# Local attention in 32-query tiles with 128 keys each, and global attention as separate tasks, in a fused attention and feed-forward kernel

## The chip, the core and the metric

The kernel runs on one core of one Trainium2 chip. The metric is the device time of one execution in microseconds. The three timed runs of the kernel before took 1042.81, 1039.39 and 1042.66 us, so the median is 1042.66 us.

## The reference, cut to what matters

There are 8 batches with 8 heads of 64 numbers each. Every head has 512 local tokens and 32 global tokens. A local query sees the 32 global keys and the local keys at most 32 positions away; a global query sees all 544 keys. The concatenated heads of the 4,352 tokens then go through a feed-forward layer of width 512 to 2048 to 512.

```python
s_g = scale * np.matmul(q_g, k_all.transpose(0, 1, 3, 2))
out_g = np.matmul(sm(s_g), v_all)                # global queries: all keys
mask = np.abs(pos[:, None] - pos[None, :]) <= 32
s_ll = np.where(mask, scale * q_l @ k_l.T, -1e9)
s_l = np.concatenate([s_lg, s_ll], axis=-1)      # 32 global keys, then local
out_l = np.matmul(sm(s_l), np.concatenate([v_g, v_l], axis=2))
h = x @ w_in                                     # x: heads side by side
g = np.maximum(h, 0.0) + alpha * np.minimum(h, 0.0)
out = g @ w_out
```

## The kernel before

**Feed-forward.** The tokens are cut into nine groups: one for the 512 local tokens of each batch, and a last one with the 256 global tokens. A group has 16 units, one for each 128 of the 2048 hidden numbers. A unit is `f1` (12 matmuls, the products of activations and weights split into a high and a low fp32r part, into a bank of tag `h`) and `f2` (12 matmuls into the four banks `o0` to `o3`, two units later, `LAG`). Between them DVE makes `g` (L407, L408), ACT its high part `gh` (L410) and POOL its low part `gl` (L411). After unit 16 ACT copies the four banks out.

**Weights.** They arrive as fp64 words. Each of 32 pieces is decoded by two ACT, three DVE (L115, L117, L118) and one POOL instruction (L120), then split by a DVE or ACT copy (L127, L129) and a POOL subtraction (L130). All pieces are decoded once, beside the attention of the first batches.

**Attention.** A pair `P` is two heads of one batch, so a batch has four pairs and there are 32 in all. A pair takes four units of the program. Pairs 0 to 7 (`NRAW`) use fp32 score matmuls of 64 queries by 160 keys (`qk_raw`), with PE transposes (L316). Pairs from 8 on use split fp32r scores with 128 queries by 192 or 224 keys (`hi`, `kl`): DVE adds the mask and takes the extreme (L246), ACT exponentiates (L250) and scales (L217), DVE transposes blocks of 32x32 (L327), and the probabilities are written to a scratch tensor in DRAM and fetched back transposed (`scratch`, `pt_sb`).

**Global queries.** The 64 global rows of a pair ride with the local ones. `global_scores` makes three matmuls per pair (`g_ps<-gn`). `global_softmax` has nine small DVE and two ACT instructions. `global_transposes` puts the result into `pt_sb` beside the local probabilities (L300, L301: 18 DVE transposes per pair from pair 8 on), so that the value matmuls of the next visit (`pv_all`, with 160 or 128 columns) give local and global outputs together.

**What sets the order.** The main loop runs over `t` from -`NPRE` = -19 to 145, and `u = t + NPRE` counts from 0. In each unit the attention pieces stand at three places: `attn_pre` ahead of `f1`, `attn_mid` between `f1` and `f2`, `attn_post` between the halves of `f2`. A scheduler orders each engine's instructions within priorities. From `u >= PIN` (36) TensorE's matmuls stay in program order. PSUM has eight banks: two of tag `h`, two of tag `s` (all attention of the later pairs) and `o0` to `o3`.

```python
for t in range(-NPRE, NT + LAG):
    ...
    attn_pre(u)
    if 0 <= t < NT: f1(t)
    attn_mid(u)
    if t >= LAG: f2(t - LAG, 0)
    attn_post(u)
    if t >= LAG: f2(t - LAG, 1)
    weights_step(u)
```

Of the kernel before, what the change touches and what calls it, by code (L numbers as in the profile page):

```python
# [17 lines left out]
NPAIR = 4  # L18
# [3 lines left out]
NQ, NK = 512, 640  # L22
NEG = -8.0e9
NKR = 704
PEC = "ad"
PEG = "da"
NWARM = 18
WARM = (2, 2)
NRAW = 8
WV = range(0, 8)  # L30
NWB = 33
NST = 18
NNP = [(0, 0), (0, 2)]
# [7 lines left out]
NPRE = 19  # L41
PIN = 36
LAG = 2
PTT = "s"
BT = dict(s="s", g="o3", o="s", w="h")
GS = (2, "mid")
EV = dict(pt0=(2, "mid"), pt1=(4, "pre"), ptg=(4, "pre"), pv0=(5, "mid"), pv1=(6, "mid"))
SM = (2, "post")
RATE = ((1, 1, 0), (2, 1))
GROUPS = [("l", b) for b in range(NB)] + [("g", 0)]  # L50

# [7 lines left out]

@with_exitstack  # L60
def longformer_ffn(ctx: ExitStack, tc: tile.TileContext, qk, qkr, gn, vt, vx, w, alpha, out):
# [35 lines left out]

    def stage(name, dtype=F32):
        return work.tile([128, 512], dtype, tag="st", name=name, bufs=NST)

    wraw, wts = {}, {}
# [4 lines left out]

    wmid = {}
# [15 lines left out]
    def split_weights(f, j):  # L123
        t = wmid.pop((f, j))
        wt = wpool.tile([128, 2, 512], F32R, tag="w", name="wt")
        if f in WV:
            nc.vector.tensor_copy(wt[:, 0, :], t)  # L127
        else:
            nc.scalar.copy(wt[:, 0, :], t)  # L129
# [10 lines left out]
    nc.vector.memset(rmask[0:64, 0, 0:32], NEG)  # L140
    nc.vector.memset(rmask[64:128, 2, 128:160], NEG)

    ident = stage("ident")[:, 0:128]
    make_identity(nc, ident)

    idle = stage("idle", F32R)
    nc.vector.memset(idle.bitcast(F32), 0.0)

    def keep_warm(n):
        for _ in range(n):  # L150
# [54 lines left out]
    def small(name, n=2):  # L205
        return work.tile([128, n], F32, tag=name, name=name, bufs=3)
# [453 lines left out]
```

## Time and profile before

| what | value |
|---|---|
| timed runs, median | 1042.66 us |
| profiled execution, first to last instruction | 1038.9 us |
| PE busy | 992.1 us, 96% of the span, 5592 matmul records |
| DVE busy | 681.0 us, 66% |
| ACT busy | 497.4 us, 48% |
| POOL busy | 410.6 us, 40% |
| moved by DMA | 133.00 MB, 128 GB/s in the mean |
| TensorE clock granted, mean | 0.977 |

The profiled execution's own time is its span, 1038.9 us; the median of the timed runs is 3.8 us above it. A matmul in fp32 shows as two records of the trace, a matmul in fp32r as one. Matmuls overlap in the trace, so the time that one costs is read from the starts of neighbours, not from its own duration. "L93" is the helper through which every matmul is issued; tiles tell them apart: `h_ps` is `f1`, `o` is `f2`, `s_ps` local scores, `o_ps` values, `g_ps` the bank that holds global scores and the last piece of the values. A PE row is named by the matmul that it belongs to, and PEld is the load of its stationary operand.

### The profile page before, as it was taken

To read this page: it belongs to the slowest core of one execution; us is meant where nothing else is said; L and a number is where in the kernel's file an instruction comes from. 1 tells how busy PE (TensorE), PEld (TensorE's weight loads), DVE (VectorE), ACT (ScalarE), POOL (GpSimd) and SP (SyncE) were. 2 spreads that over 40 slices of the span, in tenths; PEclk is the share of its full clock that TensorE was granted. 3 is DMA by queue.
4 is the path that set the end of the run, shared out by engine and by line. 5 is a ranking of instruction groups with operands and counts; after the bars stand their busy time and mean duration, and the time that the engine had idled before them with its cause. 6 is when DMAs were issued, how large, how long until landed. Compare 5 with 4: busy or idle time off the path is not lost.

```text
span 1038.9 us, 17103 instructions
## 1 busy us (share of the span) xinstructions
PE 992.1 (96%) x5592; PEld 791.2 (76%) x5592; DVE 681.0 (66%) x2162; ACT 497.4 (48%) x1331; POOL 410.6 (40%) x330
## 2 busy tenths in 40 slices
PE   6798989898999999999999999999999999999998
PEld 3455767676888878887888788878887788888798
DVE  8987788866666766676667666776667666322322
ACT  5466466665455554455455554555455543201121
POOL 6620466663344343333444433334443431122222
PEclk9896898998999999999999999999999999999999
DMA  9454232135444554455455555445445543100010
GB/s 335 175 187 172 103 126 86 56 94 161 148 148 141 160 149 148 140 161 157 148 149 151 165 150 148 141 149 151 148 144 159 146 126 92 41 1 1 1 42 21
DMA packets 95274, 133.00 MB, mean 128 GB/s; under 512 B 10192, under 2 KB 53712, under 8 KB 95184
## 3 DMA queue, kind: packets, MB, share of 16 engines
q1 hardware_dynamic: 95184, 131.91, 40.7%
q8 instruction: 44, 0.72, 0.3%
q14 instruction: 46, 0.38, 0.1%
HBM read 100.93 MB, written 30.93 MB: 127 GB/s over the span
## 4 chain that ended last, share of the span: by engine, by line
PE 77%; DVE 14%; DMA 3%; ACT 2%; issue 2%; POOL 1%; SPq 0%; ACTq 0%; DVEq 0%; POOLq 0%
PE o L93 33%; PE h_ps L93 31%; PE o_ps L93 6%; PE s_ps L93 4%; PE g_ps L93 3%; DVE wt L118 2%; DVE wt L115 2%; DVE rz L211 1%; DVE wt L117 1%; DMA rawq<-in_qk_dram 1%; DVE p_sb L246 1%; DVE g L408 1%; DMA out_dram<-ost 1%; DVE g L407 1%; DVE pt_sb L321 1%
## 5 line engine op out<-in xcount | busy, mean ns | idle before, releaser
L93 PE MATMUL h_ps<-xh,wt 128*128 128x512 f32 (+1 forms) x1152 | 352.2, 389 | 4.3 <-DVE g L408 3.9
L411 POOL TENSOR_TENSOR gl<-g,gh 128x512 fp32r<-128x512 f32 (+1 forms) x144 | 178.2, 1237 | 436.8 <-ACT gh L410 405.1
L93 PE MATMUL o<-gh,wt 128*128 128x512 f32 (+1 forms) x1152 | 282.4, 386 | 1.6 <-ACT ost L305 1.6
L93 PEld LDWEIGHTS o<-gh,wt 128*128 128x128 f32 x1152 | 204.5, 188 | 50.3 <-ACT ost L305 6.6
L93 PEld LDWEIGHTS h_ps<-xh,wt 128*128 128x128 f32 x1152 | 207.3, 191 | 44.6 <-DVE g L408 4.1
L93 PE MATMUL h_ps<-xl,wt 128*128 128x512 f32 (+1 forms) x576 | 222.6, 388 | 0.9 <-DVE xl L390 0.9
L410 ACT CAST gh<-g 128x512 fp32r<-128x512 f32 (+1 forms) x144 | 85.9, 596 | 266.4 <-DVE g L408 243.2
L407 DVE TENSOR_SCALAR g<-h_ps,alpha_sb 128x512 f32<-128x512 f32 (+1 forms) x144 | 103.2, 717 | 121.2 <-PE h_ps L93 120.4
L217 ACT ACTIVATE p_sb<-p_sb,rz 128x192 f32<-128x192 f32 (+1 forms) x252 | 101.3, 451 | 131.8 <-DVE rz L212 129.7
L93 PE MATMUL o<-gl,wt 128*128 128x512 f32 (+1 forms) x576 | 150.6, 382 | 0.0
L250 ACT ACTIVATE p_sb<-p_sb,mn 128x224 f32<-128x224 f32 (+2 forms) x256 | 115.0, 451 | 40.3 <-DVE mn L246 39.8
L93 PEld LDWEIGHTS h_ps<-xl,wt 128*128 128x128 f32 x576 | 109.3, 190 | 25.6 <-issue 1.3
L93 PEld LDWEIGHTS o<-gl,wt 128*128 128x128 f32 x576 | 104.5, 187 | 23.8 <-issue 0.5
L211 DVE TENSOR_SCALAR rz<-z 128x2 f32<-128x2 f32 x128 | 52.5, 411 | 91.3 <-ACT p_sb L250 90.2
L300 DVE STREAM_TRANSPOSE pt_sb<-sg_sb 32x64 f32<-32x64 f32 x384 | 90.7, 236 | 27.4 <-ACT sg_sb L283 21.2
L408 DVE SCALAR_TENSOR_TENSOR g<-h_ps,g 128x512 f32<-128x512 f32 (+1 forms) x144 | 93.9, 652 | 2.9
L196 POOL TENSOR_TENSOR hi<-rawq,hi 64x512 fp32r<-64x512 f32 x48 | 62.2, 1295 | 83.4 <-DMA vt<-in_vt_dram 50.0
L93 PE MATMUL o_ps<-pt_sb,vt 128*64 128x160 f32 (+4 forms) x832 | 72.3, 298 | 11.9 <-DVE mn L246 8.0
L199 POOL TENSOR_TENSOR kl<-rawk,hi 128x640 fp32r<-128x640 f32 x48 | 76.2, 1587 | 3.7
L93 PEld LDWEIGHTS o_ps<-pt_sb,vt 128*64 128x64 f32 (+2 forms) x832 | 50.3, 140 | 32.5 <-issue 12.2
L246 DVE CUSTOM_DVE_ANT_0 p_sb<-s_ps,mask 128x192 f32<-128x192 f32 x192 | 64.1, 362 | 11.1 <-PE s_ps L93 9.9
L120 POOL TENSOR_TENSOR wt<-wt,wr 128x512 int32<-128x512 int32 x32 | 43.2, 1352 | 66.2 <-DVE rz L211 38.1
(86 smaller groups left out, 1042.3 us busy)
## 6 DMA issues: line engine op xcount, KB each, us to landing
scratch<-p_sb SPq DMA_DIRECT2D x192, 112.0 KB, 2.3
wraw<-in_w_dram SPq DMA_DIRECT2D x32, 512.0 KB, 6.9
vt<-in_vt_dram SPq DMA_DIRECT2D x32, 512.0 KB, 5.0
rawk<-in_qk_dram SPq DMA_DIRECT2D x96, 160.0 KB, 2.9
rawq<-in_qk_dram SPq DMA_DIRECT2D x96, 128.0 KB, 2.7
pt_sb<-scratch SPq DMA_DIRECT2D x48, 256.0 KB, 2.8
gn<-in_gn_dram SPq DMA_DIRECT2D x32, 304.0 KB, 5.4
pt_sb<-scratch SPq DMA_DIRECT2D x48, 192.0 KB, 2.9
```

Of the source, the lines that this page charges most:

```text
L93: ins = nc.tensor.matmul(*a, **k)
L196: nc.gpsimd.tensor_tensor(q, raw[64:128], q.bitcast(F32), op=ALU.subtract)
L199: nc.gpsimd.tensor_tensor(kl[P, h], raw, t.bitcast(F32), op=ALU.subtract)
L211: nc.vector.tensor_scalar(rz[:parts, 0:n], z[:parts, 0:n], 1e-9, None, op0=ALU.add)
L217: nc.scalar.activation(r, r, AF.Copy, scale=rz[:parts, e : e + 1])
L246: nc.vector.tensor_tensor_reduce(out=pr, in0=s[:, 256 * e : 256 * e + nn], in1=masks[e], scale=-0.125, scalar=3.0e38, op0=ALU.add, op1=ALU ...
L250: nc.scalar.activation(pr, pr, AF.Exp, bias=mn[:, e : e + 1], scale=-1.0, accum_out=z[:, e : e + 1])
L300: nc.vector.transpose(dst, src)
L407: nc.vector.tensor_scalar(g[:, 0:n], h[:, 0:n], 0.0, alpha_sb[:, f : f + 1], op0=ALU.min, op1=ALU.mult)
L408: nc.vector.scalar_tensor_tensor(g[:, 0:n], h[:, 0:n], 0.0, g[:, 0:n], op0=ALU.max, op1=ALU.add)
L410: nc.scalar.copy(gh[:, 0:n], g[:, 0:n])
L411: nc.gpsimd.tensor_tensor(gl[:, 0:n], g[:, 0:n], gh[:, 0:n].bitcast(F32), op=ALU.subtract)
```

## The change

The attention is written anew; the feed-forward functions `f1` and `f2` stay as they are (`f1` is now at L279, its DVE lines at L291 and L292, ACT L294, POOL L295).

Local attention of every pair now works on blocks of 32 queries with the 128 keys that start at `window(i)` of a re-laid key sequence: 32 fp32 matmuls with 64x32 tiles per pair, one head in rows 0 to 63 and the other in rows 64 to 127 of the array, each head into its own bank (`s_ps`). The softmax runs on 128x512 tiles; eight PE transposes of 128x128 follow two units later, and 32 value matmuls (128 keys, 64 numbers, 32 queries) one unit after that. The fp32r split of queries and keys and the DRAM scratch go. Key and value blocks are laid out by the host and loaded by one and two DMAs per pair.

Global attention is a task of its own: scores and softmax (`global_scores`) between `f1` and `f2` of unit 16 + 17k/5 for pair `k`, and two units later, at the same place, `global_values`: two PE transposes, a DVE copy, two small DVE transposes (L265) and ten value matmuls.

The first batch's four pairs start every two units from `t = -10`; the weights are decoded at half a piece per unit before `t = 0` and at two pieces per unit from there on, in another order.

```diff
-NRAW = 8
...
-NPRE = 19
-PIN = 36
+NPRE = 10
+PIN = 16
...
-        if P < NRAW:
-            vxs[P] = stage("vx").rearrange("p (i n) -> p i n", i=4)
-            nc.sync.dma_start(vxs[P], vx[P])
+    def load_qk(P):
+        qks[P] = work.tile([128, SL + KS], F32, tag="qk", name="qk", bufs=2)
+        nc.sync.dma_start(qks[P], qk[P])
...
+    def local_scores(P):
+        t = qks.pop(P)
+        tags = ("o0", "o1", "o2", "o3") if P < NPAIR else ("s", "s", "s", "s")
+        for h in range(2):
+            ps_of[P, h] = bank(tags[2 * (P % 2) + h], "s_ps")
+        for i in range(NWIN):
+            for h in range(2):
+                hs = slice(64 * h, 64 * h + 64)
+                k0 = SL + window(i)
+                r0, c0 = 32 * (i % 4), 128 * (i // 4)
+                matmul(ps_of[P, h][r0 : r0 + 32, c0 : c0 + 128], t[hs, 32 * i : 32 * i + 32], t[hs, k0 : k0 + 128], start=True, stop=True)
+    def local_softmax(P):
+        for h in range(2):
+            s = ps_of.pop((P, h))
+            p = stage("p")
+            p3 = p.rearrange("q (i n) -> q i n", i=4)
+            mn, z, rz = small("mn"), small("z"), small("rz")
+            nc.vector.scalar_tensor_tensor(p, s, -0.125, mask.rearrange("q i n -> q (i n)"), op0=ALU.mult, op1=ALU.add)
+            nc.vector.tensor_reduce(mn, p3, axis=AX.X, op=ALU.min)
+            for i in range(4):
+                nc.scalar.activation(p3[:, i], p3[:, i], AF.Exp, bias=mn[:, i : i + 1], scale=-1.0, accum_out=z[:, i : i + 1])
+            nc.vector.tensor_scalar(rz, z, 1e-9, None, op0=ALU.add)
+            nc.vector.reciprocal(rz, rz)
+            eng = nc.gpsimd if P < NPAIR and h == 0 else nc.vector
+            eng.tensor_tensor(p3, p3, sub_ap(rz, 0, 128, 0, ((1, 4), (0, 128))), op=ALU.mult)
+            pr_of[P, h] = p
+    def local_transposes(P):
+        for h in range(2):
+            p = pr_of.pop((P, h))
+            ps = bank("s", "pt")
+            for i in range(4):
+                transpose(ps[:, 128 * i : 128 * i + 128], p[:, 128 * i : 128 * i + 128], ident)
+            pt_of[P, h] = stage("pt")
+            copy("ad"[h], pt_of[P, h], ps)
+    def local_values(P):
+        b, p = divmod(P, NPAIR)
+        o = bank("h" if P < NPAIR else "s", "o_ps")
+        for i in range(NWIN):
+            v = vws[P, i % 2][:, i // 2]
+            for h in range(2):
+                q = slice(32 * i, 32 * i + 32)
+                matmul(o[64 * h : 64 * h + 64, q], v[:, 64 * h : 64 * h + 64], pt_of[P, h][:, q], start=True, stop=True)
+        if P < NPAIR:
+            xs[0, p] = split(o, SL)
+        else:
+            nc.scalar.copy(x_raw[:, p], o)
...
-    def transpose_q(h):
-        pr = p_sb[:, 896 * h : 896 * h + 896]
-        nc.vector.transpose(pr, pr)
...
-    def fetch_pt(h):
...
+    def global_values(P):
+        b, p = divmod(P, NPAIR)
+        ps = bank("s", "gt")
+        for e in range(2):
+            transpose(ps[:, 128 * e : 128 * e + 128], sg_sb[:, 128 * e : 128 * e + 128], ident)
+        nc.vector.tensor_copy(sgt_sb[:, 0:4].rearrange("k (r e) n -> k r e n", r=2), ps[:, 0:256].rearrange("k (e r n) -> k r e n", e=2, r=2))
+        for h in range(2):
+            nc.vector.transpose(sgt_sb[0:32, 4, 32 * h : 32 * h + 32], sg_sb[32 * h : 32 * h + 32, 256:288])
+        v = vgs.pop(P)
+        for y in range(5):
+            for h in range(2):
+                matmul(ps[64 * h : 64 * h + 64, 256:288], v[:, y, 64 * h : 64 * h + 64], sgt_sb[:, y, 32 * h : 32 * h + 32], start=(y == 0), stop=(y == 4))
+        nc.scalar.copy(x_glb[:, p, SG * b : SG * b + SG], ps[:, 256:288])
...
+    for P in range(NPR):
+        base = 2 * P - NPRE if P < NPAIR else 4 * (P - NPAIR)
+        plan(base, "pre", local_scores, P)
+        plan(base, "pre", local_softmax, P)
+        plan(base + 2, "pre", local_transposes, P)
+        plan(base + 3, "pre", local_values, P)
...
+    for k in range(NPR):
+        t = 16 + (17 * k) // 5
+        plan(t - 2, "post", load_global, k)
+        plan(t, "mid", global_scores, k)
+        plan(t + 2, "mid", global_values, k)
...
-        weights_step(u)
+        weights_step(2 if t >= 0 else u % 2 if u < NPRE else 1)
```

The prediction speaks of two places in the order that results. The first is on PE, in the units from `t = 16` on, where the global task meets the feed-forward stream. Before, this is the visit of one pair's values with the next pair's global scores (`o_ps`, `g_ps`), between the `h_ps` of one unit and the `o` (accumulators `o0` to `o3`, with their buffer number) of another:

```order
L93 MATMUL h_ps<-xl,wt 128x512
L93 MATMUL o_ps<-pt_sb,vt 64x160 x2
L93 MATMUL o_ps<-pt_sb,vt 64x128 x2
L93 MATMUL o_ps<-pt_sb,vt 64x160 x2
L93 MATMUL o_ps<-pt_sb,vt 64x128 x2
L93 MATMUL o_ps<-pt_sb,vt 64x160 x2
L93 MATMUL o_ps<-pt_sb,vt 64x128 x2
L93 MATMUL g_ps<-pt_sb,vt 64x160 x4
L93 MATMUL g_ps<-gn 64x256 x2
L93 MATMUL g_ps<-gn 64x32
L93 MATMUL o_2688<-gh,wt 128x512 x2
```

After the change, on PE, at the same place of a unit (`gt` is the bank of the global transposes and of the global values, `sgt_sb` the transposed probabilities in SBUF that a DVE copy fills from it):

```order
L78 MATMUL h_ps<-xl,wt 128x512
L84 MATMUL gt<-ident,sg_sb 128x128 x2
L78 MATMUL gt<-sgt_sb,vg 64x32 x10
L78 MATMUL o_2274<-gh,wt 128x512 x2
L78 MATMUL o_2275<-gh,wt 128x512 x2
L78 MATMUL o_2276<-gh,wt 128x512 x2
L78 MATMUL o_2277<-gh,wt 128x512 x2
L78 MATMUL o_2274<-gl,wt 128x512
L78 MATMUL o_2275<-gl,wt 128x512
L78 MATMUL o_2276<-gl,wt 128x512
L78 MATMUL o_2277<-gl,wt 128x512
L78 MATMUL o_ps<-pt,vw 64x32 x32
```

What moved: the values of the global rows left the columns of the local ones; they follow their transposes with no other matmul between, and the local values stand in a visit of their own half a unit later.

The second place is on DVE, in the same stage. Before, the transposes of the global rows (L300, L301) stand among the softmax of the local pairs, and only the next visit's value matmuls read them:

```order
L300 STREAM_TRANSPOSE pt_sb<-sg_sb 32x64 x5
L211 TENSOR_SCALAR rz<-z 128x2
L300 STREAM_TRANSPOSE pt_sb<-sg_sb 32x64 x3
L301 STREAM_TRANSPOSE pt_sb<-sg_sb 32x32
L300 STREAM_TRANSPOSE pt_sb<-sg_sb 32x64 x3
L212 RECIPROCAL rz<-rz 128x2
L300 STREAM_TRANSPOSE pt_sb<-sg_sb 32x64 x5
L301 STREAM_TRANSPOSE pt_sb<-sg_sb 32x32
L407 TENSOR_SCALAR g<-h_ps,alpha_sb 128x512
```

After, on DVE (`rz`, `p`: softmax of a local pair; L291 and L292: `g` of the unit):

```order
L195 RECIPROCAL rz<-rz 128x4
L197 TENSOR_TENSOR p<-p,rz 128x512
L291 TENSOR_SCALAR g<-h_ps,alpha_sb 128x512
L263 COPY sgt_sb<-gt 128x256
L292 SCALAR_TENSOR_TENSOR g<-h_ps,g 128x512
L99 COPY pt<-pt 128x512
```

What moved: the copy that the global value matmuls need (L263) stands behind the first instruction of `g` (L291), which reads the `h_ps` that PE has just finished.

More of the change, by code (lines that the diff above doesn't have):

```diff
@@ L96, in matmul, with transpose, small, copy @@
         return ins
+    def transpose(*a):
+        ins = nc.tensor.transpose(*a)
+        if pinned[0]:
+            tc.keep_in_program_order(ins)
+        return ins
     def stage(name, dtype=F32):
         return work.tile([128, 512], dtype, tag="st", name=name, bufs=NST)
-    wraw, wts = {}, {}
+    def small(name, n=4):
+        return work.tile([128, n], F32, tag=name, name=name, bufs=4)
+    def copy(engine, dst, src):
+        if engine == "a":
+            nc.scalar.copy(dst, src)
+        else:
+            nc.vector.tensor_copy(dst, src)
+    def bank(tag, name):
+        return psum.tile([128, 512], F32, tag=tag, name=name, bufs=2 if tag in "hs" else 1)
+    nc.gpsimd.memset(mask, 0.0)
+    for wd in range(4):
+        lo = mask[32 * wd : 32 * wd + 32, :, 0:32]
+        nc.gpsimd.affine_select(out=lo, in_=lo, compare_op=ALU.is_ge, fill=NEG, base=0, pattern=[[0, 4], [1, 32]], channel_multiplier=-1)
+        up = mask[32 * wd : 32 * wd + 32, :, 96:128]
+        nc.gpsimd.affine_select(out=up, in_=up, compare_op=ALU.is_ge, fill=NEG, base=0, pattern=[[0, 4], [-1, 32]], channel_multiplier=1)
+    nc.vector.memset(mask[0:32, 0, 0:32], NEG)
+    nc.vector.memset(mask[96:128, 3, 96:128], NEG)
+    make_identity(nc, ident)
+    nc.vector.memset(sgt_sb, 0.0)
+    idle = stage("idle", F32R)
+    nc.vector.memset(idle.bitcast(F32), 0.0)
+    def keep_warm(n):
+        for _ in range(n):
+            ps = bank("h", "warm")
+            matmul(ps, idle[:, 0:128], idle, start=True, stop=True)
+    wraw, wmid, wts = {}, {}, {}
     def load_weights(f, j):
@@ L140, in longformer_ffn @@
[L140 to L150, printed above, removed]
-            ps = psum.tile([128, 512], F32, tag=BT["w"], name="warm", bufs=2 if BT["w"] in "hs" else 1)
-            matmul(ps, idle[:, 0:128], idle, start=True, stop=True)
-    raws, vts, vxs, gns = {}, {}, {}, {}
@@ L397, in f1 @@
         n = SL if GROUPS[G][0] == "l" else NB * SG
-        h = psum.tile([128, 512], F32, tag="h", name="h_ps", bufs=2)
+        h = bank("h", "h_ps")
         k = 0
@@ L418, in f2 @@
         if f == 0 and part == 0:
-            obs[G] = [psum.tile([128, 512], F32, tag=f"o{m}", name=f"o{m}", bufs=1) for m in range(NC)]
+            obs[G] = [bank(f"o{m}", f"o{m}") for m in range(NC)]
         o = obs[G]
@@ L534, in longformer_ffn, with attention, weights_step @@
+    for k in range(NPR):
[3 more added lines that the diff above has]
+        plan(t + 2, "mid", global_values, k)
+    def attention(t, where):
+        for fn, P in at.pop((t, where), ()):
+            fn(P)
+    pieces = sorted(((f, j) for f in range(NF) for j in range(2)), key=lambda x: x[0] + 1.5 * x[1])
     state = [0]
[L536 removed]
+    done = []
+    def weights_step(n):
         k = state[0]
[L538 to L539 removed]
+        new = list(range(k, min(k + n, len(pieces))))
```

442 lines of the change are left out of this document (83 added, 359 removed).

## The prediction

> **What bounds the kernel now.** The page was read first: busy time, then the engines of the chain that ended last, then the GB/s of 40 slices of 26 us.
>
> ```profile
> PE 992.1 (96%) x5592; PEld 791.2 (76%) x5592; DVE 681.0 (66%) x2162; ACT 497.4 (48%) x1331; POOL 410.6 (40%) x330
> PE 77%; DVE 14%; DMA 3%; ACT 2%; issue 2%; POOL 1%; SPq 0%; ACTq 0%; DVEq 0%; POOLq 0%
> GB/s 335 175 187 172 103 126 86 56 94 161 148 148 141 160 149 148 140 161 157 148 149 151 165 150 148 141 149 151 148 144 159 146 126 92 41 1 1 1 42 21
> ```
>
> PE is the chain on average, but not everywhere, so the windows by stage come next. The first ends where unit 16 begins (the PE timeline has its `h_ps` there), the third is one batch of 16 units, the last begins with the global group.
>
> ```profile
> 228.54 0.40 PE L93 MATMUL h_ps<-xh,wt 128*128 128x512 f32 x1
> ...
> core 0: us, PE busy (x) PEld busy (x) DVE busy (x) ACT busy (x) POOL busy (x), PEclk, DMA share, GB/s
> 8.00:228.50 220.50, 197.94 (x1186) 137.09 (x1185) 184.25 (x545) 134.41 (x369) 118.36 (x91) 0.91 0.42 145
> 20.00:60.00 40.00, 30.25 (x168) 18.62 (x164) 39.15 (x98) 16.86 (x47) 26.38 (x21) 0.87 0.66 241
> 590.16:700.43 110.27, 108.38 (x601) 88.50 (x601) 76.06 (x260) 57.63 (x157) 43.67 (x32) 1.00 0.50 150
> 982.40:1038.90 56.50, 51.31 (x409) 49.80 (x408) 17.61 (x38) 10.03 (x25) 12.83 (x17) 1.00 0.08 29
> ```
>
> Up to 228.5 us DVE sets the pace: 0.84 busy over the stretch, 39.15 of 40 us at its densest. From there PE does, at 108.38 of 110.27 us per batch, and DVE (0.69) has room. The chain inside that batch gives PE's prices.
>
> ```profile
> 589.10 1.06 PE g_ps L93 x14
> 590.16 2.99 PE o L93 x12
> 593.15 0.42 PE s_ps L93 x4
> 593.57 2.81 PE h_ps L93 x12
> 596.38 2.79 PE o L93 x12
> 599.17 0.44 PE s_ps L93 x4
> ```
>
> A half unit is 2.80 us, so 16 units are 89.6 us. The `o` after a value visit is 0.20 longer: leaving small tiles costs that.
>
> **What a visit costs on PE.** The new attention on PE exists in no trace, so its price is built from the timeline. Rows around one score visit (64x64 tiles), the two ends of one visit of values and global scores, and one row of transposes:
>
> ```profile
> 182.00 0.39 PE L93 MATMUL h_ps<-xl,wt 128*128 128x512 f32 x1
> 182.32 0.76 PE L93 MATMUL s_ps<-qk_raw 64*64 64x160 f32 x8
> 183.01 0.50 PE L93 MATMUL h_ps<-xh,wt 128*128 128x512 f32 x1
> ...
> 283.29 0.39 PE L93 MATMUL h_ps<-xl,wt 128*128 128x512 f32 x1
> ...
> 286.30 0.73 PE L93 MATMUL o<-gh,wt 128*128 128x512 f32 x2
> ...
> 199.55 0.66 PE L316 MATMUL pt<-ident,p_sb 128*128 128x128 f32 x4 [0.30 <-ACT sg_sb L278]
> 199.96 0.70 PE L93 MATMUL o<-gh,wt 128*128 128x512 f32 x2
> ```
>
> An fp32 matmul makes two passes, and two matmuls in different column halves run side by side. A feed-forward matmul takes 2.80/12 = 0.23, so the first visit is 183.01 - 182.00 - 0.23 = 0.78 us for 4 passes of 160 = 640 columns. The second is 286.30 - 283.29 - 0.23 = 2.78 us; its order is shown above, 16 value matmuls and three global ones, which side by side make 1728 + 640 + 576 = 2944 columns. The difference gives 2.00/2304 = 0.87 ns a column and leaves 0.22 us for entering. With 0.20 for leaving, a visit costs 0.42 us beside its columns. A pair costs 2.98 for this visit and 4 x 0.43 for the scores; four pairs and 89.6 make 108.4 of the batch's 110.3, and 1.9 stay for the group's edge.
>
> *Local scores.* 32 matmuls on 64x32 tiles: eight tiles fill the array. If eight run side by side, 4 groups x 2 passes x 128 columns x 0.87 ns = 0.89, with the visit 1.31 us. If only two do, as is all that the trace shows, 3.97. I take 1.31, since a second tile in the rows above costs no columns at all; 3.97 stays as a rival. The Trainium skill (TensorE: Matmul & The Clock Gate, Part 3: Packing small matmuls) says that row and column tiles run concurrently, about 4 ns apart; by it the sum is the one that I take, and no run here shows more than two.
>
> *Transposes.* (199.96 - 199.55)/4 = 0.10 each, eight and 0.1 around them: 0.92.
>
> *Values.* 32 matmuls of 32 columns, two side by side: 32 passes. By columns 0.89. But each pass needs 64 columns of weights first: the fp32r score matmuls above take 0.107 each (0.43/4) though their 192 or 224 columns at 0.233/512 ns are only 0.095 in the mean, so I read 0.107 as the load of 128 weight columns, an estimate, and half for 64. 32 x 0.053 + 0.42 = 2.13, kept against 1.31.
>
> A pair is then 1.31 + 0.92 + 2.13 = 4.36 us, against 4.70 now. Little is gained on PE.
>
> *Global task.* Scores: 512 columns, 0.44, and two short passes, 0.11, with a visit of their own 0.97. Then `global_values`: two transposes 0.21, ten passes of 0.053, a visit 0.42, and a wait. PE stands still between transposes and values until DVE's copy, which comes behind L291. The rows of a unit without attention, and the DVE copy of 128x256 from PSUM:
>
> ```profile
> 900.89 0.39 PE L93 MATMUL h_ps<-xl,wt 128*128 128x512 f32 x1
> 901.12 1.33 PE L93 MATMUL o<-gh,wt 128*128 128x512 f32 x5
> 901.39 0.75 DVE L407 TENSOR_SCALAR g<-h_ps,alpha_sb 128x512 f32<-128x512 f32 x1 [4.19 <-PE h_ps L93]
> 902.18 0.69 DVE L408 SCALAR_TENSOR_TENSOR g<-h_ps,g 128x512 f32<-128x512 f32 x1
> ...
> 1034.47 0.42 DVE ost L307
> ```
>
> PE would have its transposes done by 901.12 + 0.34 = 901.46; DVE is free at 902.18 and has copied at 902.60, PE goes on at about 902.65: a wait of 1.2 us. If the copy went first it would be 0.4, if L292 were ahead too, 1.9. Behind the waiting PE stand the `o` matmuls of the unit, so the whole stream is late by it. `global_values` is 0.21 + 0.53 + 0.42 + 1.2 = 2.36, a global task 3.33 us. Before, most of this was free: its values were extra columns of the local ones.
>
> A batch of 16 units holds 16/3.4 = 4.7 such tasks: 89.6 + 1.9 + 4 x 4.36 + 4.7 x 3.33 = 124.6 us instead of 110.3. DVE, ACT, POOL and the loads stay below PE there: the DRAM round trip, POOL's `kl` and `hi`, and DVE's 18 transposes per pair go, all of which had been covered by PE. Losing them gains nothing. By the sizes in the code a pair and its global task load 2.4 MB, so 9.5 MB a batch in place of 16.5 (110.3 us at 150 GB/s); no wait of PE for a load is in the window now, and none is added to the sum. The two `s` banks are taken in turn by scores, transposes, values and the global task: a bank is read out within the half unit that follows in every sequence but one, scores right after global scores, where DVE's reduction and ACT's exponential of the 128x288 bank end about when PE asks; I cost that at nothing, and at 0.3 us a batch if it is late.
>
> **The first stage.** Here DVE's work counts, up to unit 16. Rows of its instructions:
>
> ```profile
> L407 DVE TENSOR_SCALAR g<-h_ps,alpha_sb 128x512 f32<-128x512 f32 x128 | 95.5, 746 | 89.6 <-PE h_ps L93 88.8
> L408 DVE SCALAR_TENSOR_TENSOR g<-h_ps,g 128x512 f32<-128x512 f32 x128 | 87.1, 681 | 2.4
> L118 DVE SCALAR_TENSOR_TENSOR wt<-wraw,wt 128x512 uint32<-128x512 uint32 x32 | 29.9, 936 | 0.4
> L117 DVE TENSOR_SCALAR wt<-wt 128x512 uint32<-128x512 uint32 x32 | 22.0, 688 | 0.5
> L115 DVE TENSOR_SCALAR wt<-wt 128x512 f32<-128x512 f32 x32 | 21.3, 664 | 10.0 <-ACT wt L113 9.8
> L127 DVE CAST wt<-wt 128x512 fp32r<-128x512 f32 x16 | 9.9, 621 | 0.1
> L390 DVE TENSOR_TENSOR xl<-x_raw,xh 128x512 fp32r<-128x512 f32 x32 | 23.5, 743 | 1.8 <-ACT xh L389 1.6
> L307 DVE COPY pt_sb<-pt 128x512 f32<-128x512 f32 x8 | 5.4, 680 | 0.0
> L212 DVE RECIPROCAL rz<-rz 128x2 f32<-128x2 f32 x128 | 20.6, 161 | 2.9
> L273 DVE TENSOR_REDUCE gm<-g_ps 128x1 f32<-128x288 f32 x32 | 14.4, 448 | 5.2 <-PE g_ps L93 5.0 <-issue 0.2
> L379 DVE TENSOR_REDUCE x_glb<-o_ps 128x32 f32<-128x96 f32 x24 | 6.2, 258 | 27.2 <-ACT x_raw L376 27.2
> L211 DVE TENSOR_SCALAR rz<-z x128: 144/171/1543, 10.8 to 870.9; 128x2 f32<-128x2 f32 x128
> ```
>
> 32 pieces x (0.664 + 0.688 + 0.936) = 73.2; 16 copies 9.9; 16 units x 1.427 = 22.8. Pairs 0 to 7 have 16 heads with a masked add (0.68 by L408), a reduction of 512 (0.67, on the line through 96 and 288 columns), and two small ones (0.17, 0.16): 26.9. Twelve products by `rz` (the other four are POOL's) at 0.743 are 8.9, eight copies 5.4, eight `xl` 5.9. Together 153 us, where the window before had 184; gone are the global softmax and its transposes, which now come later. DVE starts at 8 us. At 0.84 busy it ends at 190, at 0.98 at 164; I take 0.90, since two pieces per unit load it without a break: unit 16 begins at 178 us, 50 earlier. PE would need 89.6 + 4 x 4.36 = 107 us from about 50 us on (10 MB of loads stand ahead of pair 2's queries on SP's queue, 30 us at the first slice's 335 GB/s, then two pairs), so it is not the bound.
>
> **The sum.** 178 + six batches with pairs 8 to 31, 6 x 124.6 = 747.6, + batch seven with 32 - 28.2 = 3.8 global tasks and no pair, 104.2, + the global group, unchanged, 56.5 = 1086.3 us of span. The median before lies 3.8 above its span, so 1090 us.
>
> **Rivals.** *Not slower: DVE is never late.* If its decode stands clear of POOL and the copy at L263 comes as soon as the transposes are done, the first stage is PE's (157, 21 less) and no wait is left (32 x 1.2 = 38): 1031. It must save 47 to reach 1043. For it: the shortest L211 is 144 against 1543 ns, so DVE can run much freer. Against it: L291 stands ahead of L263 in the order.
>
> *Score tiles go two at a time:* 24 pairs x 2.66 = 64 more, 1154. Nothing in the trace excludes it.
>
> *Instructions, not columns, set PE's pace.* The long visit had 38 records in 2.78 us, 0.07 each; at that, scores and values with 64 records each would cost 3.6 and 2.8 more, 24 x 6.4 = 154, and 20 records of global values 0.9 x 32 = 28: 1272 at most. The Trainium skill (TensorE: Matmul & The Clock Gate, "Wait — 56ns, not 53.3ns?") has starts never under 25 ns; by it the scores alone cost 1.6 instead of 0.89, and the sum would be 1107. The trace does not decide.
>
> **The numbers.** About 0.5% is what a measurement of this kernel can tell from no change. Forecast (1045 to 1130) 0.70, DVE never late 0.13 (faster), between this and the forecast 0.05 (same), two tiles at a time 0.08, instruction pace 0.04. The range 1042 to 1160 leaves out the first rival and the last. So faster 0.13, same 0.06, slower 0.81.
>
> **What would show it.** Right: unit 16 near 178 us; batches of 124 to 125 us; PE idle ahead of `gt<-sgt_sb` with release by DVE L263, about 1.2 us 32 times; an `s_ps` visit near 1.3 us, an `o_ps` visit near 2.1. Wrong: batches of 117 or less, or unit 16 before 140; a batch over 135 would mean that the score tiles don't share the array.

## The result, and the profile after

The kernel after takes 1086.63 us in the median of four runs (1083.33 to 1088.76); before, run beside it, took 1041.98. The ratio is 1.0434, with a 95% interval of 1.0404 to 1.0464: slower, and 3.4 us under the forecast. The profiled execution has a span of 1081.5 us. First the page: busy time, the engines of the chain that ended last, and the busy tenths of DVE and POOL in 40 slices of 27 us.

```profile
PE 1016.3 (94%) x8752; PEld 804.9 (74%) x8752; DVE 573.9 (53%) x1206; ACT 338.0 (31%) x995; POOL 281.0 (26%) x227
PE 76%; DVE 16%; issue 3%; ACT 2%; DMA 1%; POOL 1%; SPq 0%; DVEq 0%; POOLq 0%; ACTq 0%
DVE  4579999844445445554454544644453444433322
POOL 2248777421111121211112112112111212111222
```

Every engine but PE has less to do than before, and the kernel is slower: PE's chain has grown. The windows by stage read as follows now: they are the start up to 60 us, the stretch from there to unit 16, and one batch; the busy times stand in the order of the prediction's windows (PE, PEld, DVE, ACT, POOL). The row ahead of them, from the timeline, has the first `h_ps` of unit 16.

```profile
202.50 0.73 PE L78 MATMUL h_ps<-xh,wt 128*128 128x512 f32 x2 [0.56 <-ACT xh L213]
...
8.00:60.00 52.00, 42.29 (x556) 29.83 (x557) 28.69 (x56) 22.70 (x82) 14.63 (x12) 0.70 0.89 295
60.00:202.50 142.50, 131.58 (x942) 92.42 (x939) 135.24 (x177) 66.94 (x160) 101.28 (x72) 0.89 0.34 119
443.00:564.70 121.70, 115.47 (x1071) 92.21 (x1068) 59.34 (x141) 36.36 (x117) 21.09 (x16) 1.00 0.31 93
```

Unit 16 begins at 202.5 us, not at 178. The first six batches after it take 122.4, 118.1, 121.8, 119.6, 118.0 and 122.1, in the mean 120.3 us, not 124.6. The two errors have opposite signs and nearly cancel. What the visits cost on PE is read from the timeline of a batch:

```profile
457.70 1.03 PE L84 MATMUL pt<-ident,p 128*128 128x128 f32 x8
458.49 0.71 PE L78 MATMUL h_ps<-xh,wt 128*128 128x512 f32 x2
...
461.40 0.73 PE L78 MATMUL g_ps<-gn 128*64 128x256 f32 x6
462.06 2.11 PE L78 MATMUL o<-gh,wt 128*128 128x512 f32 x8
...
465.01 2.06 PE L78 MATMUL o_ps<-pt,vw 128*64 128x32 f32 x64
467.00 0.50 PE L78 MATMUL h_ps<-xh,wt 128*128 128x512 f32 x1
...
472.66 1.16 PE L78 MATMUL s_ps<-qk 64*32 64x128 f32 x64
473.75 0.73 PE L78 MATMUL h_ps<-xh,wt 128*128 128x512 f32 x2
```

From the start of a visit to the start of the feed-forward matmul behind it these are 0.79, 0.66, 1.99 and 1.09 us; taken from the start of the matmul ahead, less the 0.233 that a feed-forward matmul took before, they are 0.79, 0.75, 2.07 and 1.17. Then the place that the prediction put its largest wait on, the global values, on DVE and on PE at one of the 32 tasks, and the waits of the whole kernel:

```profile
602.84 0.75 DVE L291 TENSOR_SCALAR g<-h_ps,alpha_sb 128x512 f32<-128x512 f32 x1 [1.52 <-PE h_ps L78]
603.51 0.41 DVE L263 COPY sgt_sb<-gt 128x256 f32<-128x256 f32 x1
...
603.98 0.78 PE L78 MATMUL gt<-sgt_sb,vg 128*64 128x32 f32 x20 [0.96 <-DVE sgt_sb L263]
```

```profile
PE gt L78 <- DVE sgt_sb L263: 34.1, 32, 2.4
```

PE stands idle for the copy 32 times, 34.1 us in all or 1.07 each, in the order that was foreseen: L291, then L263, then PE. At 29 of the tasks the wait is 0.96 to 1.03 us; at two it is 2.3, because DVE is still at a local pair's reductions (L191) when L291 could begin.

### The profile page after: what moved, and what is told of

It is laid out like the page before. It is cut to its first block, busy times and chain, and to the rows that moved or that the text cites. A ratio compares the mean times of both kernels' runs of the same rounds, so it can differ in the third digit from the quotient of the medians.

```text
span 1081.5 us, 21173 instructions
## 1 busy us (share of the span) xinstructions
PE 1016.3 (94%) x8752; PEld 804.9 (74%) x8752; DVE 573.9 (53%) x1206; ACT 338.0 (31%) x995; POOL 281.0 (26%) x227
## 4 chain that ended last, share of the span: by engine, by line
PE 76%; DVE 16%; issue 3%; ACT 2%; DMA 1%; POOL 1%; SPq 0%; DVEq 0%; POOLq 0%; ACTq 0%
PE h_ps L78 31%; PE o L78 31%; PE o_ps L78 5%; DVE g L291 3%; PE pt L84 3%; DVE wt L138 2%; PE s_ps L78 2%; PE gt L78 2%; DVE wt L135 2%; PE g_ps L78 2%; DVE xl L214 1%; DVE p L190 1%; DVE wt L147 1%; DVE sgt_sb L263 1%; ACT p L193 1%
## 5 line engine op out<-in xcount | busy, mean ns | idle before, releaser
L295 POOL TENSOR_TENSOR gl<-g,gh 128x512 fp32r<-128x512 f32 (+1 forms) x144 | 186.0, 1292 | 713.5 <-ACT gh L294 489.8
L291 DVE TENSOR_SCALAR g<-h_ps,alpha_sb 128x512 f32<-128x512 f32 (+1 forms) x144 | 103.6, 719 | 319.4 <-PE h_ps L78 296.0
L294 ACT CAST gh<-g 128x512 fp32r<-128x512 f32 (+1 forms) x144 | 85.6, 594 | 449.3 <-DVE g L292 369.8
L193 ACT ACTIVATE p<-p,mn 128x128 f32<-128x128 f32 x256 | 99.2, 389 | 103.8 <-DVE mn L191 87.2
L292 DVE SCALAR_TENSOR_TENSOR g<-h_ps,g 128x512 f32<-128x512 f32 (+1 forms) x144 | 94.5, 656 | 2.5
L78 PEld LDWEIGHTS o_ps<-pt,vw 128*64 128x64 f32 x2048 | 67.4, 146 | 13.9 <-issue 9.8
L78 PE MATMUL o_ps<-pt,vw 128*64 128x32 f32 x2048 | 71.2, 230 | 1.8 <-DVE pt L99 1.8
L190 DVE SCALAR_TENSOR_TENSOR p<-s_ps,mask 128x512 f32<-128x512 f32 x64 | 41.1, 683 | 49.4 <-PE s_ps L78 49.3
L78 PE MATMUL s_ps<-qk 64*32 64x128 f32 x2048 | 53.3, 295 | 5.5 <-DMA qk<-in_qk_dram 3.5
L78 PE MATMUL gt<-sgt_sb,vg 128*64 128x32 f32 x640 | 24.8, 225 | 34.1 <-DVE sgt_sb L263 34.1
L78 PEld LDWEIGHTS s_ps<-qk 64*32 64x32 f32 x2048 | 35.6, 113 | 28.4 <-issue 18.0
L197 DVE TENSOR_TENSOR p<-p,rz 128x512 f32<-128x512 f32 x60 | 53.4, 891 | 1.9
L78 PEld LDWEIGHTS gt<-sgt_sb,vg 128*64 128x64 f32 x640 | 21.2, 137 | 41.7 <-DVE sgt_sb L263 41.7
```

What stands on the lines that cost most here:

```text
L78: ins = nc.tensor.matmul(*a, **k)
L190: nc.vector.scalar_tensor_tensor(p, s, -0.125, mask.rearrange("q i n -> q (i n)"), op0=ALU.mult, op1=ALU.add)
L193: nc.scalar.activation(p3[:, i], p3[:, i], AF.Exp, bias=mn[:, i : i + 1], scale=-1.0, accum_out=z[:, i : i + 1])
L197: eng.tensor_tensor(p3, p3, sub_ap(rz, 0, 128, 0, ((1, 4), (0, 128))), op=ALU.mult)
L291: nc.vector.tensor_scalar(g[:, 0:n], h[:, 0:n], 0.0, alpha_sb[:, f : f + 1], op0=ALU.min, op1=ALU.mult)
L292: nc.vector.scalar_tensor_tensor(g[:, 0:n], h[:, 0:n], 0.0, g[:, 0:n], op0=ALU.max, op1=ALU.add)
```

## The experiments

The theory of the sum was: a visit's price on PE and the wait for L263 set the batches, DVE's work sets the first stage. Two points of the trace of after spoke against parts of it from the start: unit 16 came 24.5 us late, and feed-forward matmuls of 512 columns started 227 ns apart in the median, against 234 before. In the runs that follow, the median of before beside them was 1039.2 to 1040.5 us.

**Before, once more.** No edit.

> The kernel before, unchanged, beside the variants on one chip. After the change a feed-forward matmul of 512 columns starts every 227 ns where the kernel before had 234 ns (medians of the starts of neighbours from unit 16 on). Theory A, the step belongs to the kernel (where its tiles lie): 234 ns here again, and 227 ns in the variants of the changed kernel on the same chip. Theory B, the step belongs to the chip or the run: one and the same step in all four.

1038.53 us, and the feed-forward step is again 234 ns; the variants of after that kept the global tiles and ran beside it have 227. So 234 and 227 belong to the kernels and not to the occasion.

**No wait between global transposes and global values.** The transposes and the copy stay where they are, the ten products go half a unit further on, behind eight `o` matmuls.

```diff
+        gts[P] = ps
+
+    def global_products(P):
+        b, p = divmod(P, NPAIR)
+        ps = gts.pop(P)
         v = vgs.pop(P)
...
         plan(t + 2, "mid", global_values, k)
+        plan(t + 2, "post", global_products, k)
```

> The changed kernel with the global value matmuls moved behind eight feed-forward matmuls (1.8 us), so that the copy is done when they come. Theory, PE's stream pays for each wait: the 2.04 us visit falls to about 0.3 for the transposes and 0.75 for the values, 32 x 1.0 = 32 us less than the changed kernel, about 1054 us. Rival, the wait is taken back elsewhere (another engine or a bank is late by as much): under 10 us less, 1077 or more.

1051.26 us, ratio 1.0084 (1.0054 to 1.0115) against before: 35.4 us less than after, near the theory's 32 and far from the rival's 10. The batches are 113.9 to 117.3 us. PE's waits from unit 16 on have this row where they had the 34.1 us:

```profile
PE gt L78 <- DVE sgt_sb L263: 1.0, 2, 0.5
```

The wait for L263 was worth about what the waits view said, 34.1 us: PE was the chain there, and no other engine took its place.

**The copy on ACT instead of DVE.**

```diff
-        nc.vector.tensor_copy(sgt_sb[:, 0:4]...
+        nc.scalar.copy(sgt_sb[:, 0:4]...
```

> The changed kernel with the copy of the transposed global probabilities on ACT in place of DVE, all else the same. Theory, 0.75 us of each wait is the g instruction L291 ahead of the copy on DVE: the visit falls from 2.04 to about 1.3 us, 32 x 0.75 = 24 us less, about 1062 us. Rival, the wait is transposes, copy and their hand-overs by themselves: within 5 us of the changed kernel, 1082 to 1091.

1085.22 us, ratio 1.0433 (1.0402 to 1.0464): no change. In the median the visit falls from 2.04 to 1.55 us, but the mean only from 2.15 to 1.98, since at some tasks the copy now stands in ACT's queue. In the waits the row of the copy, then one such task on PE and on ACT:

```profile
PE gt L78 <- ACT sgt_sb L263: 27.6, 32, 2.4
```

```profile
449.05 0.44 PE L84 MATMUL gt<-ident,sg_sb 128*128 128x128 f32 x2
451.85 1.25 PE L78 MATMUL gt<-sgt_sb,vg 128*64 128x32 f32 x20 [2.37 <-ACT sgt_sb L263]
```

```profile
450.28 0.40 ACT L193 ACTIVATE p<-p,mn 128x128 f32<-128x128 f32 x1 [3.52 <-DVE mn L191]
...
451.06 0.39 ACT L193 ACTIVATE p<-p,mn 128x128 f32<-128x128 f32 x1
...
451.45 0.35 ACT L263 COPY sgt_sb<-gt 128x256 f32<-128x256 f32 x1
```

The transposes are done by 449.5. ACT stands still until 450.28, since the exponential at its head waits for DVE's reduction L191; only behind three of these comes the copy. The waits fall by 6.5 us and the kernel gains 1.4, inside the spread of its runs. One queue was exchanged for another. So the time fits the rival, but its reason does not: where ACT is free the visit is 0.5 us shorter, so L291 is part of the wait.

**No global attention.** The three calls per pair are left out.

```diff
+    nc.vector.memset(x_glb, 0.0)
...
-        plan(t - 2, "post", load_global, k)
-        plan(t, "mid", global_scores, k)
-        plan(t + 2, "mid", global_values, k)
```

> The changed kernel without its global attention: no global loads, scores, softmax or values, zeros in the activations of the global tokens; the feed-forward of the global group stays. Theory, each global task costs PE its two visits, 0.95 + 2.24 us: 32 x 3.2 = 102 us less, about 984 us, and batches of 104 to 105 us. Rival, half of the tasks' time would be idle time of PE anyway: 40 to 60 us less, 1025 to 1045.

995.74 us in a single run, 91 less than after, in batches of 106.6 us: nearer to the theory's 102 than to the rival's 40 to 60. The step is 232 ns here, which takes back 5 of 7 ns on each feed-forward matmul, 13 us over seven batches, and unit 16 comes 5 us later than in after.

**Score tiles in another order.** The same 32 matmuls, with neighbours that write the same rows of the array's output.

```diff
-        for i in range(NWIN):
+        for i in [4 * c + r for r in range(4) for c in range(4)]:
```

> The changed kernel with its 32 score matmuls of a pair in another order: four that share a column tile follow each other, so only the two heads (row tiles) can run side by side. Theory, tiles share the array if their rows or columns differ and the next one is at hand: the visit rises from 1.17 us to 16 x 2 passes x 128 columns x 0.87 ns = 3.6 us, 23 visits, about 55 us more than the changed kernel, 1140 us. Rival, the order is nothing to PE (it picks tiles out of its queue, or the weights' loads set the pace): 1.2 us, 1087 us.

1112.74 us in a single run. The score visit of this kernel in the timeline:

```profile
485.41 2.48 PE L78 MATMUL s_ps<-qk 64*32 64x128 f32 x64
487.83 0.73 PE L78 MATMUL h_ps<-xh,wt 128*128 128x512 f32 x2
```

2.42 us in place of 1.09. So the 1.17 us of after rest on tiles that run side by side, which the prediction had only assumed; with the good order eight records start within 50 ns. The other end of the expectation was wrong: with the sharing hindered it is 2.50 by the measure above, not 3.6, so some of it remains.

**Decoding casts off DVE.** From here on the first stage. If DVE paces it, 16 casts fewer must bring unit 16 forward.

```diff
-        if j:
-            nc.vector.tensor_copy(wt[:, 0, :], t)
-        else:
-            nc.scalar.copy(wt[:, 0, :], t)
+        nc.scalar.copy(wt[:, 0, :], t)
```

> The changed kernel with all 32 first halves of the weight split on ACT; before, 16 of them are DVE copies of 1.30 us in the mean, 20.8 us of DVE before unit 16. Theory, DVE paces units 0 to 16 (135 of 142 us busy): unit 16 begins 15 to 20 us earlier than 202.5, about 1068 us. Rival, POOL or the order of the pieces paces them: unit 16 moves by less than 5 us, 1082 or more.

1084.83 us, ratio 1.0423 (1.0371 to 1.0476); unit 16 at 201.4 us. DVE lost 11.9 us of its work in that stretch and nothing moved:

```profile
60.00:201.40 141.40, 130.45 (x978) 93.32 (x976) 123.30 (x162) 75.48 (x176) 102.19 (x73) 0.92 0.36 121
```

The theory that DVE's own work is the pace falls with this.

**Fewer weights ahead.** `AHEAD = 2` in place of 6.

> The changed kernel with two weight pieces loaded ahead of need instead of six, so that 2.1 MB less stand before the first batch's queries on SP's queue. Theory, the first 62 us are set by loads (DVE busy 29 of 52 us): unit 0 and unit 16 begin 5 to 7 us earlier, about 1080 us. Rival, the first 62 us are the chain of the four pairs (scores, softmax, transposes, values one behind the other) and not the loads: unit 0 moves by less than 2 us, and later pieces that come late can cost: 1086 to 1095 us.

1099.82 us, ratio 1.0556 (1.0518 to 1.0595). Unit 0 comes at 74.4 and unit 16 at 220.4 us, where after had 62.7 and 202.5: neither side's gain. From 40 to 50 us this kernel loads nothing, where after loads at 280 GB/s; with fewer pieces ahead the loads themselves stop. So this run does not tell whether the loads or the chain of the first four pairs set the first 62 us.

**Global attention merged into the local visits.** One task every four units; its scores stand right behind the local values, its transposes half a unit ahead of the next such visit, its products in that visit.

```diff
+    def slot(k):
+        return 15 + 4 * k if k < 25 else 111 + 2 * (k - 24)
...
-        plan(t - 2, "post", load_global, k)
-        plan(t, "mid", global_scores, k)
-        plan(t + 2, "mid", global_values, k)
+        t, nxt = slot(k), slot(k + 1)
+        plan(slot(k - 1) if k else t - 2, "post", load_gn, k)
+        plan(t, "post", load_vg, k)
+        plan(nxt - 1, "mid", global_values, k)
+        plan(nxt, "pre", global_products, k)
+        plan(t, "pre", global_scores, k)
```

> The changed kernel with the global task spread over the local one's places: its transposes half a unit after the local transposes, its values and the next pair's scores directly behind the local values, all three with 128x64 tiles. Theory, no wait is left (32 x 1.2) and 25 of the visits share their entry and exit (25 x 0.84): 1087 - 38 - 21 = about 1027 us, below the kernel before. Rival, the banks that three tasks need at one place bring new waits of 1 us or more each: 1045 to 1060 us.

1029.52 us, ratio 0.9906 (0.9879 to 0.9933): about 1% less than before, as the theory had it. Transposes, then the visit that follows:

```profile
448.35 0.38 PE L84 MATMUL gt<-ident,sg_sb 128*128 128x128 f32 x2
448.48 2.09 PE L78 MATMUL o<-gh,wt 128*128 128x512 f32 x8
...
451.41 2.06 PE L78 MATMUL o_ps<-pt,vw 128*64 128x32 f32 x64
453.29 0.75 PE L78 MATMUL gv<-sgt_sb,vg 128*64 128x32 f32 x20
453.88 0.71 PE L78 MATMUL g_ps<-gn 128*64 128x256 f32 x6
454.52 0.73 PE L78 MATMUL h_ps<-xh,wt 128*128 128x512 f32 x2
```

The transposes cost 0.13 us and no wait, and the three in one visit take 3.20 us where apart they took 2.07, 0.75 and, with transposes and wait, 2.15. The batches fall to 110.5 us.

**Program order from unit 0.** In after, the scores of pairs 4 to 7 stand one by one among f1's matmuls; between the starts of units 0 and 16 they take 19.8 us of PE. `PIN = 0` gathers them again.

> After with one number changed: PIN = 0, so that TensorE's matmuls keep the order of the program from unit 0 on instead of unit 16. In after the score matmuls of pairs 4 to 7 stand one by one between f1's matmuls (s_ps takes 19.8 us of PE's starts for these four pairs, where four visits of 1.17 would take 4.7). Theory P (PE paces units 0 to 16, and the mixing of tiles costs it): s_ps falls to about 5 us, unit 16 begins about 15 us earlier, near 188 instead of 202.5 us, the batches from unit 16 on stay at 118 to 122 us, and the time is about 1071. Rival Q (POOL, DVE or the weights' arrival pace these units): s_ps falls as well, but PE waits where it worked before, unit 16 moves by less than 5 us and the time is 1082 to 1090. Rival R (program order makes PE wait for softmax results that the mixed order had stepped around): unit 16 comes later than 202.5 us.

1081.88 us, ratio 1.0406 (1.0373 to 1.0439). The scores fall to 9.7 us, and unit 16 comes at 200.5, 2 us earlier: rival Q. PE (the first busy time) now waits where it had worked, 24.19 of 30 us busy against 29.00 in after, and DVE and POOL (the third and fifth) go on nearly as in after, which had 29.74 and 21.37 in the first of these stretches:

```profile
90.00:120.00 30.00, 24.19 (x152) 19.31 (x151) 28.45 (x42) 14.55 (x36) 20.87 (x16) 0.89 0.47 174
120.00:150.00 30.00, 21.36 (x147) 16.59 (x146) 27.79 (x39) 14.46 (x37) 21.23 (x16) 0.89 0.34 109
```

**The merged version in program order.** The same edit on the merged version.

> The merged version (global scores behind the local values, global transposes a unit ahead of the global products, one global task every four units) with PIN = 0. Merged ran at 1029.5 with unit 16 at 209.6 us. By theory P its unit 16 comes about 15 us earlier and the time is near 1014; by rival Q the time stays within 5 us of 1029; by rival R it is above 1035.

1027.82 us, ratio 0.9884 (0.9859 to 0.9908), within 5 us of merged: rival Q again. Unit 16 is at 202.7 us. The 209.6 that the expectation compares with come from a profiled execution of merged that took 1035.83 us and began unit 0 at 68.4 us, where this one has 61.9; so 6.5 of the 6.9 us lie ahead of unit 0.

**Before, with its weights 288 bytes further on.** All engines have the instructions of before in their order; only one tile is longer.

```diff
-            raw = work.tile([128, n], F32, tag="raw", name="rawq", bufs=1)
+            raw = work.tile([128, n + 72], F32, tag="raw", name="rawq", bufs=1)[:, 0:n]
```

> Before with one tile made 288 bytes longer per partition (the raw queries, of which the first part is used as before). All five engines have the same instructions in the same order; only the weights and what lies behind that tile stand 288 bytes further on in SBUF, so that weight tiles begin at a multiple of 2048 bytes from the activation tiles, as they do in after (in before they stand 1760 bytes off that, where feed-forward matmuls start 234 ns apart, against 227 in after). Theory L (the distance in SBUF between weights and activations sets the step): the step falls from 234 to about 227 ns, 3072 matmuls of 512 columns save 7 ns each, 21 us, and the time is about 1020. Rival M (the step belongs to what else the kernel does at the time, its DMA traffic or the small tiles): 234 ns and 1038 to 1043 as before. A step that rises instead would mean that the place counts, but not by this distance.

1029.77 us, ratio 0.9903 (0.9873 to 0.9933): 9.5 us less than before. The step is 227 ns. The chain in a late batch, to be laid beside the prediction's 2.81 and 2.79:

```profile
644.06 2.76 PE h_ps L93 x12
646.82 2.72 PE o L93 x12
```

So the place of the weights in SBUF sets the step, as theory L had it, and rival M is excluded. Whether it is their distance from the activations or their own address is not told apart, since both moved by the 288 bytes. As to its size, 9.5 us came of the 21 expected: a batch falls from 110.3 to 108.8 us, and the first stage and the global group do not gain.

**The weights' subtractions on DVE.** On the merged version with `PIN = 0`. The explanation that was left for the first stage comes from two pieces of the timeline of after, DVE's and POOL's:

```profile
121.76 0.74 DVE L291 TENSOR_SCALAR g<-h_ps,alpha_sb 128x512 f32<-128x512 f32 x1
...
123.14 1.36 DVE L147 CAST wt<-wt 128x512 fp32r<-128x512 f32 x1
124.54 1.38 DVE L135 TENSOR_SCALAR wt<-wt 128x512 f32<-128x512 f32 x1
125.95 1.38 DVE L137 TENSOR_SCALAR wt<-wt 128x512 uint32<-128x512 uint32 x1
127.25 1.49 DVE L135 TENSOR_SCALAR wt<-wt 128x512 f32<-128x512 f32 x1
...
129.27 0.41 DVE L137 TENSOR_SCALAR wt<-wt 128x512 uint32<-128x512 uint32 x1
```

```profile
121.52 1.46 POOL L140 TENSOR_TENSOR wt<-wt,wr 128x512 int32<-128x512 int32 x1
122.94 2.70 POOL L150 TENSOR_TENSOR wt<-wt 128x512 fp32r<-128x512 f32 x2
125.60 1.45 POOL L295 TENSOR_TENSOR gl<-g,gh 128x512 fp32r<-128x512 f32 x1
127.02 1.44 POOL L150 TENSOR_TENSOR wt<-wt 128x512 fp32r<-128x512 f32 x1
129.49 1.32 POOL L140 TENSOR_TENSOR wt<-wt,wr 128x512 int32<-128x512 int32 x1 [1.03 <-DVE wt L138]
```

Where POOL stands still, at 129.27, L137 takes 0.41 us. Where POOL runs, DVE's instructions from SBUF end some 0.3 us behind POOL's: the one from 125.95 at 127.33, beside POOL's from 125.60 to 127.05; the one from 127.25 at 128.74, beside POOL's from 127.02 to 128.46. L291, which reads PSUM, takes its 0.74 beside POOL's from 121.52 as well.

```diff
-        nc.gpsimd.tensor_tensor(wt[:, 1, :], t, wt[:, 0, :].bitcast(F32), op=ALU.subtract)
+        nc.vector.tensor_tensor(wt[:, 1, :], t, wt[:, 0, :].bitcast(F32), op=ALU.subtract)
```

> The merged version with PIN = 0 (1027.8 us, unit 16 at 202.7 us), and the 32 subtractions that make the low part of a weight moved from POOL to DVE (POOL 1437 ns each between 62 and 202 us; DVE's subtraction of the same size and from SBUF was 677 ns in before while POOL was idle, and up to 1059 beside it). Theory S (in units 0 to 16 POOL and those DVE instructions that stretch beside it exclude each other, so their times add): now POOL's 98.8 us and about 33 us of DVE's decoding, casts and products, at their lengths without POOL, fill 132 of the 140 us; then POOL has 58 and DVE 52, and unit 16 begins 15 to 22 us earlier, at 181 to 188 us; the batches from there on stay as they are (110.6 us) and the time is 1006 to 1013. Rival D (DVE's own work paces the stage, POOL does not count): DVE has 28 x 0.68 = 19 us more to do, unit 16 begins near 222 us and the time is about 1047. Rival W (the weights' arrival or PE paces it): unit 16 stays within 5 us of 202.7 and the time within 5 us of 1028.

1020.56 us, ratio 0.9818 (0.9796 to 0.9840), the lowest time of these kernels. Unit 16 comes at 196.6 us, 6.1 earlier. Units 0 to 16 of the version without and with the edit, with the cast's row of each:

```profile
61.90:202.70 140.80, 114.20 (x918) 89.02 (x916) 132.26 (x184) 65.28 (x160) 99.39 (x72) 0.90 0.37 123
...
L147 DVE CAST wt<-wt 128x512 fp32r<-128x512 f32 x15 | 11.6, 776 | 1.2 <-POOL wt L140 1.2
```

```profile
61.60:196.60 135.00, 111.36 (x924) 87.99 (x916) 130.19 (x212) 66.42 (x160) 65.14 (x44) 0.92 0.38 129
...
L150 DVE TENSOR_TENSOR wt<-wt 128x512 fp32r<-128x512 f32 x28 | 26.7, 963 | 0.1
...
L147 DVE CAST wt<-wt 128x512 fp32r<-128x512 f32 x15 | 9.5, 635 | 0.0
```

DVE has 26.7 us of subtractions more and is busy 2.1 us less, because its other rows shrink when POOL has less to do: L147 as shown, and L135 from 30.2 to 20.9 us. That excludes rival D, by which unit 16 would be 19 us later. The gain is over the 5 us that rival W allowed, but only by 1 to 2 us. Theory S keeps its direction and a third of its size: the subtractions stretch on DVE too, from 0.68 to 0.96 us, and DVE stays at 0.96 busy.

## Why the prediction was right, and where it was not

| term | predicted | measured | difference |
|---|---|---|---|
| first stage, to unit 16 | 178 | 202.5 | +24.5 |
| six batches | 747.6 | 721.9 | -25.7 |
| batch seven | 104.2 | 99.8 | -4.4 |
| global group to the end | 56.5 | 57.2 | +0.7 |
| span | 1086.3 | 1081.5 | -4.8 |

**The total: in part luck.** The direction and the wait came as foreseen, but the 24.5 us that the first stage was too short and the 30.1 that the seven batches were too long have separate causes. That they left 4.8 us of the span, and 3.4 of the time, is luck.

**The mechanism of the slowdown: right.** The copy behind L291 stops PE, 1.07 us against the 1.2 taken, and with that stop taken away 35 of the 45 us are back. Losing POOL's and DVE's old work in the batches could gain little, as said: in the prediction's batch of before PE had waited 1.9 us in all for other engines.

**The visits: right.** Without what leaving costs, a pair was put at 3.96 us and measured at 1.17 + 0.79 + 2.07 = 4.03; a task at 2.93 and measured at 0.79 + 2.15 = 2.94. The rule of columns, taken from tiles of 64x64, held for tiles of 64x32. For the short passes of 32 columns the estimate of 0.053 us came out as (2.07 - 0.22)/32 = 0.058; that loading their weights is what sets it was not tested. For tiles side by side the Trainium skill (TensorE: Matmul & The Clock Gate, Part 3: Packing small matmuls) had the answer that the trace of before lacked: they run concurrently. By that rule the score visit is the 1.31 of the sum; the trace agrees, at 1.17 and 0.1 for leaving.

**The batches: mis-sized by the feed-forward part.** The feed-forward with edge and leaving costs was put at 124.6 - 4 x 3.96 - 4.7 x 2.93 = 95.0 us of a batch; the same remainder of the measured 120.3 is 120.3 - 4 x 4.03 - 4.7 x 2.94 = 90.4. Of these 4.6 us the step is 384 x 7 ns = 2.7: the prediction carried 2.80 us per half unit over as a constant, and the place of the weights in SBUF changes it. The rest lies in leaving a visit (0.10 to 0.18 rather than 0.20: the matmul behind a visit starts some 100 ns late) and the group's edge. Before, moved, shows that a kernel with the old instructions gains 9.5 us by the place alone, so the change's own instructions cost nearer to 54 than to 45 us; this difference rests on two kernels, and what exactly 7 ns bring in the first stage of after was not measured.

**The first stage: the step that failed.** It said: DVE's work, 153 us, starts at 8 us and goes at 0.90. Two things were wrong with it. Up to 60 us DVE could not work at that share: 28.69 of 52 us, while the loads ran at 295 GB/s, where 0.90 would have made 46.8. The prediction had put PE's start at 50 us for the loads and the first pairs and did not hold DVE to it. That is 18.1 us of work carried past 60 us. What held DVE is shown only in part: its longest wait there, 7.5 us, is for scores whose queries landed at 34 us; the others are waits for ACT and PE inside the chain of the first pairs. And its work came to 28.69 + 135.24 = 163.9 us, 11 more than counted, since rows that wait for POOL are longer (L147 was counted at 0.621 us and takes 1.31 in the mean). At the 0.95 that DVE then reached (135.24 of 142.5) these two cost 29.1/0.95 = 30.6 us; being at 0.95 rather than 0.90 for the 106 us that were left in the sum gives 6 back. That makes 24 of the 24.5. This divides the error up and is no test of it.

The engine that is busy throughout is then DVE, as predicted, but that time is not all DVE's own work. Three rows of it from 60 us to unit 16 (the last numbers are busy us, the mean ns of one, and idle us before):

```profile
L138 DVE SCALAR_TENSOR_TENSOR wt<-wraw,wt 128x512 uint32<-128x512 uint32 x28 | 31.9, 1141 | 0.4
L135 DVE TENSOR_SCALAR wt<-wt 128x512 f32<-128x512 f32 x28 | 25.5, 912 | 0.1
L147 DVE CAST wt<-wt 128x512 fp32r<-128x512 f32 x15 | 19.7, 1314 | 0.3
```

Beside a running POOL instruction the median of L135 is 1.48 us and alone 0.415, of L147 1.48, of L138 1.65 against 0.68, while L190, L191, L291 and L292 are the same with and without. Each row's time over its length alone, summed from 60 us to unit 16, makes 53 of DVE's 135 us. The prediction's sum put nothing on POOL in this stage beyond the mean lengths of the old rows; POOL is busy for 101 of the 142.5 us. This would explain why taking 16 casts from DVE moved nothing, and the last run shows it in part. The Trainium skill (SBUF — State Buffer, Who interferes with whom) states it as an exclusive lock between VectorE and GpSimd on one pair of ports, held for a whole instruction, for copies, casts and `tensor_scalar` in a two-port mode and for instructions with two SBUF inputs against a GpSimd instruction that reads SBUF. The trace agrees with its list in every row named here. What limits the stage once POOL has 65 us of work is open: DVE is at 0.96 there, with 33 us of such time left by the same count.

That PE "is not the bound" there held: gathering the scores gave PE 10 us and the stage 2.

**The rivals.** *DVE is never late* asked for no wait and a first stage of PE's pace; neither came. *Two tiles at a time* is excluded, by 1.17 us per visit and by the reordered tiles. *Instructions set PE's pace* is excluded too: 64 records of a score visit start within 0.9 us, some 14 ns each, where this rival needed 70 and its lighter form 25.

**The cheap alternative was in the order.** The merged version does the same arithmetic with the same tiles as after; it lets other matmuls stand between transposes and products and makes one visit of three, and is 57 us faster than after. Against before it wins nothing in all by its instructions: before with its weights moved takes 1029.77 us, merged 1029.52, at the same step of 227 ns.

## What to carry to other kernels

A new short task on the engine that bounds costs its matmuls, its entering and leaving, and each wait inside it: put other work between the halves of a chain across engines, and append its matmuls to a visit that is made anyway. Where DVE and POOL both work from SBUF, do not count the busier one alone: here 53 of DVE's 135 us were time added beside POOL, though adding up the two in full foresaw three times the gain that the last run brought. For the start of a kernel hold every engine, not only the last, to the arrival of its data. A constant taken from the trace of one kernel, even the step of a matmul, can move with the layout: check it in the new trace before you explain a few per cent by anything else.

## What the runs showed of the hardware that was not expected

- The step of a 512-column fp32r matmul depends on where the weights stand in SBUF, by their own address or relative to the activations: 227 ns when the tiles are a multiple of 2048 bytes apart (after, and before moved), 234 at 1760 bytes off it (before), 232 without the global tiles, at 896 off it. In the global group it goes the other way, 120 against 118 ns at 256 columns. Three distances do not make a rule, and why it is so was not found.
- Score tiles of 64x32 that share rows of the output one after the other still overlap: a visit takes 2.42 us, where 3.6 were expected and the good order takes 1.09.
- DVE's casts and decoding steps of 128x512 from SBUF (L135, L137, L147) take 0.41 us alone and up to 1.5 beside POOL, L138 with its two inputs 0.68 and up to 1.68; L190, L291 and L292, which read PSUM, and the reduction L191 take the same time with and without.
